# Query-layout heads that keep their exponentials in PSUM, with every low half subtracted on VectorE

## The chip, the cores and the metric

The kernel runs on one core of a Trainium2 chip. A core has a matrix engine (TensorE, PE in the profile, with PEld for its weight loads), a vector engine (VectorE, DVE), an activation engine (ScalarE, ACT), a general engine (GpSimd, POOL) and a queue engine (SyncE, SP) that issues most DMAs here. They run side by side, each in the order of its own program, and wait for one another through semaphores. SBUF is the working memory; PSUM is the memory that TensorE writes its products to. The metric is the time of one execution on the device in microseconds; several runs are taken and the median is used.

## The reference, cut to what matters

Attention over 4 batches of 8 heads, 768 positions, 64 dimensions, in which a query sees only the keys with the same six hash bits; then a gated layer with a spatial product over the positions.

```python
q_bits = (np.einsum('bhsd,dk->bhsk', q, proj) > 0)     # six bits of a position; k_bits likewise
mask = q_bucket[:, :, :, None] == k_bucket[:, :, None, :]
scores = np.where(mask, scale * (q @ k.T), -1e9)
attn = np.exp(scores - scores.max(-1))
x = attn / (attn.sum(-1) + 1e-9) @ v                   # heads side by side: 512 columns
h = np.maximum(x @ w_in, 0)
u, v = h[..., :512], h[..., 512:]
v_n = (v - v.mean(-1)) / np.sqrt(v.var(-1) + 1e-6)
v_s = np.einsum('ts,bsd->btd', w_spatial, v_n) + b_spatial[None, :, None]
out = (u * v_s) @ w_out
```

## The kernel before

There are 32 heads, n = 0 to 31, each with six tiles i of 128 rows. Heads 1 to 7 (`KEYS`) are *key-layout*: their scores come out with the keys on the partitions, their exponentials are used as they are (L265), and a separate pass finds the row maxima (L243). The other 25 heads, 0 and 8 to 31, are *query-layout*, and only they are touched here. The kernel keeps single-precision accuracy by splitting numbers into a 16-bit high part and a 16-bit low part; products are then made of three 16-bit matmuls.

A query-layout tile goes through this ring, all in `scores` and `weighted`:

- L291 and L292 on PE: four matmuls write the scores of 128 queries against 768 keys into a PSUM tile `ps` (`sp` in the trace). The pool `ps_sc` has two such buffers (`PSB[0]`), used in turn by query tiles, key tiles and the row maxima.
- L293 on DVE: the negated row maximum `nb`, with the scaled scores written to a throw-away tile `jk`.
- L295 on ACT: the exponential, from PSUM to an SBUF tile `ex` (three buffers, `EB`).
- L298 on ACT: the high half, `ex` rounded to 16 bits, into `pp[:, 0]` (three buffers, `PB`).
- L299: the low half, `ex` minus the high half, into `pp[:, 1]`. It runs on POOL for tiles 0 and 3 of heads below 16 (`PL_POOL1`) and for tile 2 of the later ones (`PL_POOL`), and on DVE for the others: 34 on POOL, 116 on DVE.
- L301 on SP: one DMA transposes both halves into `pt` (five buffers), so that the keys come to lie on the partitions.
- L314 to L316 on PE: 18 matmuls weigh the values with the transposed tile and add it to the head's sum `pv`.

A main loop over g = 6n + i issues the scores of one tile and the weighted sum of an earlier one (five tiles back, `LAG`), with the preparation of later heads and one or two units of the gating layer in between: `vps` (L361), `ups` (L402), `sps` (L417) and `ops` (L432), twelve or eighteen matmuls each. The gating layer of a batch follows its last head by a queue that is drawn from at a fixed rate of tiles, so the layer of batch 3 comes last, after all heads. The order on each engine isn't that of the text: a scheduler sorts all instructions by priorities that `at` gives and by when their operands are expected, and buffers that are still held count among these.

Of the kernel before, what the change touches and what calls it, by code (L numbers as in the profile page):

```python
# [11 lines left out]
F32 = mybir.dt.float32  # L12
I64 = mybir.dt.int64
U32 = mybir.dt.uint32
AF = mybir.ActivationFunctionType
ALU = mybir.AluOpType
# [3 lines left out]
P = 128  # L20
# [16 lines left out]
def lsh_attention_spatial_gating(  # L37
# [11 lines left out]
    nc = tc.nc  # L49
    B, NPAIR, _, _, S = kq.shape  # L50
    NH = 2 * NPAIR
    NT = S // P
    HS = S // 2
# [4 lines left out]
    ISQ = 1.0 / (SQ * SQ * 8.0)  # L58
# [7 lines left out]
    wk = ctx.enter_context(tc.tile_pool(name="wk", bufs=1))  # L66
# [35 lines left out]
    st = {}  # L102
# [153 lines left out]
    def scores_k(n, i):  # L256
        t = ab[n % NAB]
        ps = ps_sc.tile([P, 2, 512], F32, tag="sc", name=f"sp{n}_{i}")[:, :, :HS]
        ks = slice(i * P, (i + 1) * P)
        for c in range(2):  # L260
            cs = slice(c * HS, (c + 1) * HS)
            nc.tensor.matmul(ps[:, c], lhsT=t[:, 1, ks], rhs=t[:, 0, cs], start=True, stop=False)  # L262
            nc.tensor.matmul(ps[:, c], lhsT=t[:, 2, ks], rhs=t[:, 3, cs], start=False, stop=True)  # L263
        ex = wk.tile([P, S], F32, tag="pt", bufs=PTB, name=f"ex{n}_{i}")
        st["ex", n, i] = nc.scalar.activation(ex.rearrange("p (c q) -> p c q", c=2), ps, AF.Exp, scale=ISQ).ins  # L265
        st["pt", n, i] = ex
# [11 lines left out]
    def scores(n, i):  # L278
        if n in KEYS:
            scores_k(n, i)  # L280
            return
        t = ab[n % NAB]
        if i == 0:
            st["nb", n] = wk.tile([P, NT], F32, tag="nb", bufs=3, name=f"nb{n}")
        nb = st["nb", n][:, i:i + 1]
        jk = wk.tile([P, 2, HS], BF16, tag="jk", name=f"jk{n}_{i}")
        qs = slice(i * P, (i + 1) * P)
        ps = ps_sc.tile([P, 2, 512], F32, tag="sc", name=f"sp{n}_{i}")[:, :, :HS]
        for c in range(2):
            cs = slice(c * HS, (c + 1) * HS)  # L290
            nc.tensor.matmul(ps[:, c], lhsT=t[:, 0, qs], rhs=t[:, 1, cs], start=True, stop=False)  # L291
            nc.tensor.matmul(ps[:, c], lhsT=t[0:P - 1, 3, qs], rhs=t[0:P - 1, 2, cs], start=False, stop=True)  # L292
        nc.vector.tensor_scalar(jk, ps, -ISQ, None, op0=ALU.mult, op1=ALU.min, accum_out=nb)  # L293
        ex = wk.tile([P, 2, HS], F32, tag="ex", bufs=EB, name=f"ex{n}_{i}")
        st["ex", n, i] = nc.scalar.activation(ex, ps, AF.Exp, bias=nb, scale=ISQ).ins  # L295
        at(NT * n + i + G_H, 50)
        pp = wk.tile([P, 2, 2, HS], F16, tag="pp", bufs=PB, name=f"pp{n}_{i}")
        nc.scalar.copy(pp[:, 0], ex)  # L298
        (nc.gpsimd if i in (PL_POOL if n >= 2 * NH else PL_POOL1) else nc.vector).tensor_tensor(out=pp[:, 1], in0=ex, in1=pp[:, 0], op=ALU.subtract)  # L299
        pt = st["pt", n, i] = wk.tile([P, 2 * NT, P], F16, tag="pt", bufs=PTB, name=f"pt{n}_{i}")  # L300
        st["tr"] = nc.sync.dma_start_transpose(out=pt, in_=pp.rearrange("p g c k -> p (g c k)")).ins  # L301

# [144 lines left out]
    N = B * NH  # L447
    NP = B * NPAIR

    PL_POOL = (2,)  # L450
    KEYS = {1, 2, 3, 4, 5, 6, 7}
    PL_POOL1 = (0,3)
    LAGK = 3
    LEAD = 4
    MQ = nc.sync
# [7 lines left out]

    RB = 3
    PB = 3
    EB = 3
    PTB = 5
    XTB = 6
    LAG = 5
# [15 lines left out]
    def at(g, k):  # L485
        tc.cur_priority = int(1000 * (g + 40) + k)
# [17 lines left out]
    for g in range(N * NT + LAG):  # L504
        n, i = divmod(g, NT)
        if n < N:
            at(g + G_S, 0)
            scores(n, i)
            r = n // 2
            at(g + G_P, 300)  # L510
# [103 lines left out]
```

## Time and profile before

| | |
|---|---|
| three runs, median (lowest to highest) | 736.97 us (735.91 to 740.86) |
| span of the profiled execution | 741.7 us |
| head 0 and the key-layout heads 1 to 7 | up to 173 us |
| first score matmul of head 8 to the last subtract of head 31 | 173.0 to 655.6 us |
| the gating layer after the last head, to the end | 660.6 to 741.7 us |

The page lists groups as: line, engine, operation, tile written <- tiles read, shapes, count, then busy time and the mean of one in ns, then how long the engine had been idle just before them and what ended most of that idle time. Rows of waits read: who waited <- for whom: us in total, times, longest. Rows in the order of time begin with the start and the duration in us. In the tables of windows there follow after the window and its length the busy times of PE, weight loads, DVE, ACT and POOL with the counts of instructions, then the granted TensorE clock, the share of the DMA engines' time and GB/s. Names stand without their numbers, so `pp` is any of the three buffers.

### The profile page before, as it was taken

How to read it: one execution, taken by the hardware profiler on the slowest of the kernel's cores; microseconds unless marked ns; L12 is line 12 of the kernel's file. 1: busy time of each engine (PE TensorE's matmuls, PEld its weight loads, DVE VectorE, ACT ScalarE, POOL GpSimd, SP SyncE). 2: the span in 40 equal slices, each digit the busy share in tenths (PEclk: the TensorE clock that was granted, in tenths of full speed). 3: DMA queues.
4: the chain of work that ended last, by engine and by line, in shares of the span. 5: the costliest groups of instructions: out<-in, count | busy, mean ns of one | idle time of the engine just before them, and what ended most of it. 6: DMA issues, size and time to landing. Idle time of an engine off the chain costs nothing.

```text
span 741.7 us, 14927 instructions
## 1 busy us (share of the span) xinstructions
PE 631.5 (85%) x5759; PEld 400.4 (54%) x5759; DVE 520.6 (70%) x945; ACT 434.8 (59%) x668; POOL 321.2 (43%) x324
## 2 busy tenths in 40 slices
PE   1569898998988776997898899889898998999997
PEld 0237686776445444554544555556455565654553
DVE  4677795536799999567689798678698987755200
ACT  1344574346788676655676577667677776743221
POOL 5122443123458675264314565156235571451503
PEclk9768797999999989898999999999999999999999
DMA  9565554324999989996999799999999999860011
GB/s 235 149 123 155 133 148 102 99 55 97 224 237 197 215 207 187 213 178 138 234 202 199 138 210 213 211 211 212 206 210 181 194 175 213 182 136 15 1 42 43
DMA packets 290011, 120.95 MB, mean 163 GB/s; under 512 B 270740, under 2 KB 273812, under 8 KB 289940
## 3 DMA queue, kind: packets, MB, share of 16 engines
q1 hardware_dynamic: 287636, 119.11, 76.4%
q10 hardware_dynamic: 2304, 0.89, 0.5%
q8 instruction: 45, 0.74, 0.4%
q14 instruction: 26, 0.21, 0.1%
HBM read 28.33 MB, written 6.29 MB: 47 GB/s over the span
## 4 chain that ended last, share of the span: by engine, by line
PE 43%; DMA 21%; DVE 13%; issue 8%; ACT 6%; POOL 6%; SPq 3%; ACTq 0%; DVEq 0%; POOLq 0%
DMA pt<-pp 14%; PE pv L275 6%; PE vps L361 6%; PE ops L432 5%; PE sps L417 5%; PE ups L402 5%; DMA ab<-hl 4%; PE sp L291 3%; DVE jk L293 3%; PE sp L292 3%; DVE pp L299 2%; PE sp L262 2%; PE pv L314 2%; ACT ex L295 2%; PE sp L263 2%
## 5 line engine op out<-in xcount | busy, mean ns | idle before, releaser
L295 ACT ACTIVATE ex<-sp,nb 128x768 f32<-128x768 f32 x150 | 134.1, 897 | 54.8 <-DVE jk L293 48.9
L299 DVE TENSOR_TENSOR pp<-ex,pp 128x768 f16<-128x768 f32 x116 | 126.2, 1089 | 47.6 <-ACT pp L298 46.5
L293 DVE TENSOR_SCALAR_CACHE_REDUCE jk<-sp 128x768 bf16<-128x768 f32 x150 | 142.4, 949 | 24.1 <-PE sp L292 22.2
L298 ACT CAST pp<-ex 128x768 f16<-128x768 f32 x150 | 124.3, 829 | 50.0 <-DMA pt<-pp 43.9
L314 PE MATMUL pv<-vp,pt 128*128 128x65 f16 x900 | 108.2, 198 | 40.5 <-DMA pt<-pp 40.2
L291 PE MATMUL sp<-ab 128*128 128x384 f16 x300 | 103.2, 344 | 31.6 <-ACT ex L295 19.3
L314 PEld LDWEIGHTS <-pt 128*128 128x128 f16 x900 | 86.7, 101 | 67.2 <-DMA pt<-pp 53.4
L299 POOL TENSOR_TENSOR pp<-ex,pp 128x768 f16<-128x768 f32 x34 | 58.1, 1708 | 131.1 <-ACT pp L298 124.6
L315 PE MATMUL pv<-vp,pt 128*128 128x64 f16 x900 | 108.0, 197 | 0.0
L316 PE MATMUL pv<-vp,pt 128*128 128x65 f16 x900 | 107.8, 198 | 0.0
L292 PE MATMUL sp<-ab 127*128 127x384 f16 x300 | 103.9, 346 | 0.0
L417 PE MATMUL sps<-ws,vn 128*128 128x384 f16 x576 | 100.9, 329 | 1.5 <-DVE sg L180 1.0
L315 PEld LDWEIGHTS <-pt 128*128 128x128 f16 x900 | 87.0, 100 | 11.3 <-issue 1.3
L316 PEld LDWEIGHTS <-pt 128*128 128x128 f16 x900 | 86.9, 100 | 3.1 <-issue 0.5
L417 PEld LDWEIGHTS <-vn 128*128 128x128 f16 x576 | 55.3, 99 | 37.8 <-issue 3.9
L432 PE MATMUL ops<-wo,g 128*128 128x512 f16 x288 | 70.9, 391 | 1.5 <-ACT o L436 0.9
L275 PEld LDWEIGHTS pv<-vf,ex 128*128 128x128 f32 x504 | 68.5, 208 | 4.1 <-issue 1.6
L402 PE MATMUL ups<-xt,wi 128*128 128x384 f16 x384 | 69.1, 333 | 1.3 <-ACT u L405 0.9
L361 PE MATMUL vps<-wi,xt 128*128 128x512 f16 x288 | 68.0, 383 | 1.4 <-DMA xt<-xs 1.3
L275 PE MATMUL pv<-vf,ex 128*128 128x65 f32 x504 | 67.0, 286 | 0.0
L333 POOL TENSOR_TENSOR x<-x,xf 128x384 f32<-128x384 f32 x32 | 35.5, 1110 | 64.1 <-DVE x L332 64.1
L422 POOL TENSOR_TENSOR sy<-sy,u 128x384 f32<-128x384 f32 x32 | 36.6, 1145 | 49.3 <-DVE sy L421 49.2
(87 smaller groups left out, 1010.7 us busy)
## 6 DMA issues: line engine op xcount, KB each, us to landing
qk<-kq SPq DMA_DIRECT2D x16, 768.0 KB
ab<-hl SPq DMA_DIRECT2D x31, 384.0 KB
ab<-hl SPq DMA_DIRECT2D x34, 192.0 KB
out<-o SPq DMA_DIRECT2D x24, 256.0 KB
v<-v SPq DMA_DIRECT2D x13, 384.0 KB
raw<-w_in SPq DMA_DIRECT2D x16, 256.0 KB
pt<-pp SPq DMA_TRANSPOSE x150
raw<-w_sp SPq DMA_DIRECT2D x12, 192.0 KB
```

The source lines that it names most:

```text
L275: nc.tensor.matmul(acc[:, qi, :], lhsT=ex[:, qi * P:(qi + 1) * P], rhs=vf[p % 2][:, 2 * i + e, :], start=(i == 0 and qi == 0), stop=(i == ...
L291: nc.tensor.matmul(ps[:, c], lhsT=t[:, 0, qs], rhs=t[:, 1, cs], start=True, stop=False)
L292: nc.tensor.matmul(ps[:, c], lhsT=t[0:P - 1, 3, qs], rhs=t[0:P - 1, 2, cs], start=False, stop=True)
L293: nc.vector.tensor_scalar(jk, ps, -ISQ, None, op0=ALU.mult, op1=ALU.min, accum_out=nb)
L295: st["ex", n, i] = nc.scalar.activation(ex, ps, AF.Exp, bias=nb, scale=ISQ).ins
L298: nc.scalar.copy(pp[:, 0], ex)
L299: (nc.gpsimd if i in (PL_POOL if n >= 2 * NH else PL_POOL1) else nc.vector).tensor_tensor(out=pp[:, 1], in0=ex, in1=pp[:, 0], op=ALU.subtract)
L314: nc.tensor.matmul(acc, lhsT=pt[:, c, :], rhs=vh, start=(i == 0 and c == 0), stop=False)
L315: nc.tensor.matmul(acc[:, 0:D], lhsT=pt[:, c, :], rhs=vl, start=False, stop=False)
L316: nc.tensor.matmul(acc, lhsT=pt[:, NT + c, :], rhs=vh, start=False, stop=(i == NT - 1 and c == NT - 1))
L361: nc.tensor.matmul(ps, lhsT=xt[c][:, gx, i * P:(i + 1) * P], rhs=wi[gw][:, c, F2:DF], start=(k == 0), stop=(k == 3 * NPAIR - 1))
L417: nc.tensor.matmul(ps[:, :HS], lhsT=vn[gv][:, c, d * P:(d + 1) * P], rhs=ws[gw][:, c, hs], start=(k == 0), stop=(k == 3 * NT - 1))
```

## The change

For query-layout heads the exponential is written back over the scores in PSUM, the cast and the subtract read it there, and the subtract always runs on DVE (POOL has no access to PSUM, and `PL_POOL`, `PL_POOL1` go). The SBUF tile `ex` and its three buffers go with them. The key-layout heads are as they were.

```diff
         nc.vector.tensor_scalar(jk, ps, -ISQ, None, op0=ALU.mult, op1=ALU.min, accum_out=nb)
-        ex = wk.tile([P, 2, HS], F32, tag="ex", bufs=EB, name=f"ex{n}_{i}")
-        st["ex", n, i] = nc.scalar.activation(ex, ps, AF.Exp, bias=nb, scale=ISQ).ins
+        st["ex", n, i] = nc.scalar.activation(ps, ps, AF.Exp, bias=nb, scale=ISQ).ins
         at(NT * n + i + G_H, 50)
         pp = wk.tile([P, 2, 2, HS], F16, tag="pp", bufs=PB, name=f"pp{n}_{i}")
-        nc.scalar.copy(pp[:, 0], ex)
-        (nc.gpsimd if i in (PL_POOL if n >= 2 * NH else PL_POOL1) else nc.vector).tensor_tensor(out=pp[:, 1], in0=ex, in1=pp[:, 0], op=ALU.subtract)
+        nc.scalar.copy(pp[:, 0], ps)
+        nc.vector.tensor_tensor(out=pp[:, 1], in0=ps, in1=pp[:, 0], op=ALU.subtract)
```

Lines behind L295 stand one lower in the changed kernel: the exponential is L294, the cast L297, the subtract L298, the transpose L300, and the weighted sums L313 to L315.

With the same priorities the scheduler sorts differently, since a score buffer is now held to the end of the subtract. On DVE, in head 16 before (`jk16_5` is the row maximum of head 16, tile 5; `pp16_4` the subtract of tile 4; `rv` and `x` normalize an earlier head):

```order
L293 TENSOR_SCALAR jk16_4_4164,nb16_3997<-sp16_4_4165 128x768
L328 TENSOR_SCALAR rv15_4200<-pv15_3978 128x6
L293 TENSOR_SCALAR jk16_5_4213,nb16_3997<-sp16_5_4214 128x768
L329 RECIPROCAL rv15_4200<-rv15_4200 128x6
L330 SCALAR_TENSOR_TENSOR rv15_4200<-nb15_3702,rv15_4200 128x6
L332 TENSOR_TENSOR x15_4204<-pv15_3978,rv15_4200 128x384
L293 TENSOR_SCALAR jk17_0_4277,nb17_4276<-sp17_0_4278 128x768
L299 TENSOR_TENSOR pp16_4_4173<-ex16_4_4171,pp16_4_4173 128x768
```

The same place in the changed kernel:

```order
L293 TENSOR_SCALAR jk16_4_4106,nb16_3943<-sp16_4_4107 128x768
L298 TENSOR_TENSOR pp16_3_4083<-sp16_3_4076,pp16_3_4083 128x768
L298 TENSOR_TENSOR pp16_4_4114<-sp16_4_4107,pp16_4_4114 128x768
L293 TENSOR_SCALAR jk16_5_4154,nb16_3943<-sp16_5_4155 128x768
L293 TENSOR_SCALAR jk17_0_4217,nb17_4216<-sp17_0_4218 128x768
L219 SCALAR_TENSOR_TENSOR vp1_95<-v32_9_3705,vp1_95 128x12x64
L298 TENSOR_TENSOR pp16_5_4162<-sp16_5_4155,pp16_5_4162 128x768
```

Before, the row maxima of the next two tiles stood ahead of a tile's subtract; now at most that of the next one does, and the subtracts come in pairs behind pairs of maxima.

On PE, behind the last weighted sum of the last head (`pv31`, from `pt31_5`), before (`g2` and `ops2_3` belong to the gating layer of batch 2):

```order
L315 MATMUL pv31_8675<-vp1_95,pt31_5_8673 128x64
L316 LDWEIGHTS pt31_5_8673
L316 MATMUL pv31_8675<-vp1_95,pt31_5_8673 128x65
L432 LDWEIGHTS g2_1_1_8389
L432 MATMUL ops2_3_8801<-wo0_106,g2_1_1_8389 128x512
```

The same place now (`xt15` holds the last pair of heads, `vps3_0` opens the gating layer of batch 3):

```order
L314 MATMUL pv31_8525<-vp1_95,pt31_5_8523 128x64
L315 LDWEIGHTS pt31_5_8523
L315 MATMUL pv31_8525<-vp1_95,pt31_5_8523 128x65
L360 LDWEIGHTS xt15_8647
L360 MATMUL vps3_0_8699<-wi0_102,xt15_8647 128x512
```

All of batch 2's layer now stands ahead of the last head's weighted sums, and so do the first nine of twelve matmuls of `vps3_0` and of `vps3_1`; before, 28 matmuls of `ops2_3` to `ops2_5` and all 72 of `vps3` stood behind.

More of the change, by code (lines that the diff above doesn't have):

```diff
@@ L448, in lsh_attention_spatial_gating @@
     NP = B * NPAIR
-    PL_POOL = (2,)
     KEYS = {1, 2, 3, 4, 5, 6, 7}
-    PL_POOL1 = (0,3)
     LAGK = 3
@@ L465, in lsh_attention_spatial_gating @@
     PB = 3
-    EB = 3
     PTB = 5
```

## Prediction

> **What bounds the kernel now.** I read the page's totals first, then the busy times of the long stage, then its groups and waits, and last single tiles in the order of time. A tile below is one block of 128 queries of a query-layout head; there are 150, six for head 0 and 144 for heads 8 to 31.
>
> ```profile
> span 741.7 us, 14927 instructions
> PE 631.5 (85%) x5759; PEld 400.4 (54%) x5759; DVE 520.6 (70%) x945; ACT 434.8 (59%) x668; POOL 321.2 (43%) x324
> 173.00:656.00 483.00, 417.36 (x4331) 258.02 (x4330) 394.94 (x704) 334.85 (x499) 240.80 (x219) 0.95 0.98 197
> ```
>
> The last row is the window 173 to 656 us, in which all 144 tiles run: PE is busy 417.4 of 483 us (86%), VectorE (DVE) 394.9 (82%), ScalarE (ACT) 334.9 (69%), POOL 240.8 (50%), and the DMA engines 98%. Nothing is idle enough to be called free, and DMA is nearest to full. The same window by groups and by waits:
>
> ```profile
> L293 DVE TENSOR_SCALAR_CACHE_REDUCE jk<-sp 128x768 bf16<-128x768 f32 x144 | 136.7, 949 | 19.6 <-PE sp L292 17.7
> L295 ACT ACTIVATE ex<-sp,nb 128x768 f32<-128x768 f32 x144 | 128.8, 897 | 40.6 <-DVE jk L293 34.7 <-issue 3.2 <-DMA ab<-sg 0.7
> L299 DVE TENSOR_TENSOR pp<-ex,pp 128x768 f16<-128x768 f32 x112 | 122.4, 1094 | 47.5 <-ACT pp L298 46.5 <-issue 0.3
> L298 ACT CAST pp<-ex 128x768 f16<-128x768 f32 x144 | 119.3, 829 | 49.8 <-DMA pt<-pp 43.9 <-ACT ex L295 1.3 <-ACT g L423 1.2
> L299 POOL TENSOR_TENSOR pp<-ex,pp 128x768 f16<-128x768 f32 x32 | 54.3, 1696 | 110.6 <-ACT pp L298 104.1 <-DVE jk L293 5.6 <-PE vps L361 0.9
> PE pv L314 <- DMA pt<-pp: 34.5, 29, 4.0
> PE sp L291 <- ACT ex L295: 18.9, 15, 5.1
> ```
>
> The reader sees a ring with two limits. The cast L298 waits 43.9 us for a transpose to give one of three pp buffers back, and PE 34.5 us for transposed tiles: that is the DMA side. PE waits only 18.9 us, 15 times, for an exponential to give a score buffer back: that is the PSUM side, so far nearly free. One tile with hardly a wait shows the links; the last row is the first matmul of the tile two later, which takes the same score buffer:
>
> ```profile
> 515.47 0.33 PE L291 MATMUL sp<-ab 128*128 128x384 f16 x1
> 516.76 0.95 DVE L293 TENSOR_SCALAR_CACHE_REDUCE jk<-sp 128x768 bf16<-128x768 f32 x1
> 517.92 0.89 ACT L295 ACTIVATE ex<-sp,nb 128x768 f32<-128x768 f32 x1
> 518.84 0.83 ACT L298 CAST pp<-ex 128x768 f16<-128x768 f32 x1
> 519.83 0.95 DVE L299 TENSOR_TENSOR pp<-ex,pp 128x768 f16<-128x768 f32 x1
> 520.53 0.32 PE L291 MATMUL sp<-ab 128*128 128x384 f16 x1
> ```
>
> Today the buffer is free when L295 ends, 517.92 + 0.89 - 515.47 = 3.34 us after it was taken. The matmul at 520.53 starts before the subtract ends at 520.78: that order is what the change forbids.
>
> **The change, step by step.** *The hold.* The score buffer is now released by the subtract, not by the exponential. There are two score buffers, so the time per tile cannot be under (hold + handover) / 2, where the hold runs from the first score matmul to the end of the subtract. First, last and an early undisturbed tile of the 144:
>
> ```profile
> 173.01 0.33 PE L291 MATMUL sp<-ab 128*128 128x384 f16 x1
> 177.33 1.64 POOL L299 TENSOR_TENSOR pp<-ex,pp 128x768 f16<-128x768 f32 x1 [9.53 <-ACT pp L298]
> 174.73 0.33 PE L291 MATMUL sp<-ab 128*128 128x384 f16 x1
> 180.38 1.16 DVE L299 TENSOR_TENSOR pp<-ex,pp 128x768 f16<-128x768 f32 x1
> 648.58 0.32 PE L291 MATMUL sp<-ab 128*128 128x384 f16 x1
> 654.48 1.11 DVE L299 TENSOR_TENSOR pp<-ex,pp 128x768 f16<-128x768 f32 x1
> ```
>
> From 173.01 to 654.48 + 1.11 = 655.59 it is 482.6 us, or 3.35 us a tile; so two buffers allow a hold of 6.7. Over the 144 tiles (first and last above) the distance from matmul to end of subtract is now 9.38 us on average, far over 6.7; 1.67 us of it is the cast's wait, mostly for pp. In the 32 tiles whose cast follows the exponential within 0.1 us (first 174.73, last 648.58) it is 6.83. The subtract averages 1.23 us over all 144, and 0.95 undisturbed (row at 519.83), so I take 6.83 - 0.33 = 6.50 for a tile that does not wait for pp (its own subtract averaged 1.28 there and takes 0.95). Bounds for the new hold: 5.31 (the tile at 515.47) gives 2.7 us a tile and costs nothing; 9.38 - 0.28 = 9.10 gives 4.58 and costs 1.23 x 144 = 177 us. The truth lies between: waits on PE, DVE and ACT are partly slack that a tighter order removes, but the wait for pp does not go while DMA is 98% full. I take 6.50 plus half of the 1.67, 7.34, plus 0.05 for the handover: 3.70 us a tile, so 144 x (3.70 - 3.35) = **+50 us**, nearer the lower end because 6.50 comes from whole tiles of the same kernel. Behind the waiting score matmul on PE stand the weighted sums and the gating matmuls, which wait with it; behind those, SP issues the next heads' loads in the same order as the transposes, so they slip too and cost nothing more.
>
> The Trainium skill, Perfetto Trace Analysis, Identifying Performance Opportunities, says that the same gap repeating on an engine that should be saturated can mean too few SBUF or PSUM buffers for the next tile. That speaks against this change. The trace bears it out only weakly so far, with the 18.9 us above; by the rule that row should grow several times over.
>
> *The operations.* The nearest rows for new operand places:
>
> ```profile
> L332 DVE TENSOR_TENSOR x<-pv,rv 128x384 f32<-128x384 f32 x32 | 17.8, 555 | 0.7
> L339 DVE TENSOR_TENSOR xs<-x,xs 128x384 f16<-128x384 f32 x32 | 20.1, 628 | 3.7 <-ACT xs L338 3.7
> L405 ACT ACTIVATE u<-ups 128x384 f32<-128x384 f32 x32 | 15.5, 486 | 10.5 <-PE ups L402 9.6 <-PE pv L316 0.8
> L423 ACT CAST g<-sy 128x384 f16<-128x384 f32 x32 | 16.3, 508 | 39.7 <-POOL sy L422 37.1 <-DMA ab<-sg 2.6
> L265 ACT ACTIVATE ex<-sp 128x768 f32<-128x768 f32 x42 | 33.9, 806 | 32.2 <-PE sp L263 28.9 <-PE mp L241 3.0
> 652.28 1.81 DVE L299 TENSOR_TENSOR pp<-ex,pp 128x768 f16<-128x768 f32 x1
> 652.27 1.00 POOL L333 TENSOR_TENSOR x<-x,xf 128x384 f32<-128x384 f32 x1 [0.51 <-DVE x L332]
> ```
>
> A DVE product from PSUM (L332) takes 0.555 us where the one from SBUF (L339) takes 0.628, and the subtract at 652.28 took 1.81 beside a POOL operation against 0.95 alone. So the subtract from PSUM is 0.95, bounded by 0.95 and 1.09. All 144 on DVE make 144 x 0.95 = 137 us instead of 122.4, +14; DVE's stage goes from 395 to 409 us, hidden as long as the tile time is 3.70 (DVE then 77% of 532), and up to 14 us if it is not. POOL loses 54.3 us; it waited 104.1 us for casts, so that is worth nothing by itself. The cast from PSUM: 0.83, less some 0.02 by L405 against L423, nothing. No row shows ACT writing PSUM: 0.90 as now, bounded by 0.81 (L265, without bias) and, as much above, 0.99; that is 0.09 of hold, 0.045 a tile, 6 us either way.
>
> The Trainium skill, Perfetto Trace Analysis, Optimizing Scalar/DVE Operations, gives DVE about 60 ns of access overhead on SBUF and about 125 ns on PSUM. By that the 144 subtracts would cost 144 x 65 ns, an estimate of 9 us of DVE more. L332 and L339 show no such surcharge, so the sum leaves it out.
>
> *The end.* The scheduler also moves gating matmuls. After the last weighted sum stand now:
>
> ```profile
> 660.58 6.04 PE ops L432 x28
> 666.62 15.54 PE vps L361 x72
> ```
>
> In the changed order the 28 output matmuls of batch 2 stand ahead of the last head's weighted sums, and so do 18 of the 72 that open batch 3. On the chain that ends last that is 6.04 + 18 x 15.54 / 72 = 9.9 us less; it goes into PE's idle time of the long stage (483 - 417 = 66 us). If that cover is gone it comes back whole. **-10 us**. Head 0's six tiles, by the same 0.35 us: **+2 us** (bounds 0 and 7, by 1.23 a tile).
>
> The sum is +42 us on the profiled execution's 741.7, or 783.7. The three runs have a median of 736.97 (735.91 to 740.86), 4.7 under that span; taking it off gives 779, which I round to **778**.
>
> **The rivals.** (a) *Hidden behind the transposes.* For it: DMA at 98%, 43.9 us of pp waits; a score chain that is slower where it would have waited anyway costs nothing. Against: the hold has to stay at 6.6 or less, and unhurried tiles already need 6.5. The tile time stays at 3.35 to 3.45: -8 to +6 us, 729 to 743.
>
> (b) *Faster.* 59 of the 116 DVE subtracts run beside a POOL tensor operation and average 1.22 us against 0.95 for the rest, and 34 run on POOL at 1.7. Taking this away shortens the way from cast to transpose by 59 x 0.27 + 34 x 0.75 = 41 us in total, and with three pp buffers the ring turns 41 / 3 = 14 us faster if pp is the limit; with the end's 10 that makes about 714. It decides only while the mean hold stays under 2 x 3.35 - 0.05 = 6.65 us. The Trainium skill, SBUF — State Buffer, Who interferes with whom, has the mechanism: a DVE instruction with two SBUF inputs contends with a GpSimd one that reads SBUF, one with at most one SBUF input does not. The row at 652.28 agrees.
>
> (c) *DVE becomes the bound.* 409 us at today's share of 82% make the stage 500 us, +17; with the end, 746. Against: the two-buffer ring bites first.
>
> (d) *All waits stay.* Hold 9.10, 4.58 us a tile, +177 - 8: 906. Against: slower tiles leave every engine less loaded, which shortens its queues.
>
> **How the numbers follow.** The forecast, the two-buffer ring at 3.4 to 4.0 us a tile, 742 to 825, has 0.66; (a) 0.12, (b) 0.06, (c) 0.08, (d), in full or for the larger part, 0.08. One per cent is 7 us, about what a measurement of this kernel can tell from no change. Faster by more than that (under 730): (b) and a little of (a), 0.08. Within: most of (a) and a corner of the forecast and (c), 0.10. Slower: 0.82. The range that leaves out (b), some of (a) and the worse half of (d) is 735 to 845.
>
> **What would show it.** PE's wait at L291 for the subtract (it was 18.9 us, for the exponential) should be the largest PE wait, 60 us or more; the tile time in the long stage 3.7 us; the cast's wait for pp down to half of 43.9; DMA share near 0.88 there; the subtract near 0.95 us and no longer stretched; the end 10 us shorter after the last weighted sum. It is wrong if PE's wait at L291 stays under 30 us, if DMA stays at 0.98, or if the exponential into PSUM costs clearly more than 0.99.

## The result: 12% slower, and the profile after

The changed kernel takes 825.64 us (median of 4 runs, 822.47 to 828.68) against 736.44 us (also of 4 runs, one more than in the table above); the ratio is 1.121, with a 95% interval of 1.116 to 1.126. The forecast was slower, 778 us; the time lies within its range, but the loss is 89 us where 42 were forecast. The page of the changed kernel, first its totals:

```profile
span 824.4 us, 14923 instructions
PE 666.0 (81%) x5759; PEld 410.2 (50%) x5759; DVE 520.1 (63%) x979; ACT 433.9 (53%) x668; POOL 228.5 (28%) x290
```

Every engine is a smaller share of the span than before. TensorE alone has clearly more busy time, matmuls 666.0 against 631.5 us and weight loads 410.2 against 400.4, with the same 5759 of each. So it isn't the load of one engine; something makes all of them wait. The ends of the long stage, first score matmul of head 8 and last subtract of head 31, with the window between:

```profile
177.00 0.33 PE L291 MATMUL sp<-ab 128*128 128x384 f16 x1
738.59 0.96 DVE L298 TENSOR_TENSOR pp<-sp,pp 128x768 f16<-128x768 f32 x1 [1.77 <-ACT pp L297]
177.00:740.00 563.00, 458.81 (x4423) 271.98 (x4422) 395.48 (x737) 337.93 (x504) 157.69 (x190) 0.89 0.82 171
```

The stage now takes 739.55 - 177.00 = 562.6 us, 3.91 us a tile, against 482.6 and 3.35. That is +80 of the span's +82.7; the start has +4.0, the end -1.3. The DMA engines fell from 98% to 82%: they are no longer near full. The stage by groups and by waits:

```profile
L293 DVE TENSOR_SCALAR_CACHE_REDUCE jk<-sp 128x768 bf16<-128x768 f32 x144 | 137.1, 952 | 78.2 <-PE sp L292 74.7 <-PE pv L315 1.1
L298 DVE TENSOR_TENSOR pp<-sp,pp 128x768 f16<-128x768 f32 x144 | 136.7, 952 | 43.4 <-ACT pp L297 42.9
L294 ACT ACTIVATE sp<-sp,nb 128x768 f32<-128x768 f32 x144 | 126.0, 876 | 115.0 <-DVE jk L293 114.4
L297 ACT CAST pp<-sp 128x768 f16<-128x768 f32 x144 | 114.8, 799 | 17.0 <-ACT sp L294 4.8 <-issue 3.3 <-DMA ab<-sg 3.2
PE pv L313 <- DMA pt<-pp: 67.6, 48, 4.1
PE sp L291 <- DVE pp L298: 31.8, 25, 3.6
ACT pp L297 <- DMA pt<-pp: 2.8, 4, 1.1
```

Each of the four operations is as fast as before (the row maximum within 3 ns) or faster. What grew is the waiting for the link before: VectorE 74.7 us for scores (17.7 before), ScalarE 114.4 for the maximum (34.7). The cast hardly waits for a pp buffer any more (2.8 us, last row; 43.9 before). Read from the end backwards, everybody waits for TensorE to make the next scores. But TensorE itself waits only 31.8 us for a released buffer, and 67.6 for transposes. The answer is in what it does between a release and the next scores:

```profile
620.35 0.96 DVE L298 TENSOR_TENSOR pp<-sp,pp 128x768 f16<-128x768 f32 x1 [1.93 <-ACT pp L297]
...
621.04 2.77 PE L401 MATMUL ups<-xt,wi 128*128 128x384 f16 x8
623.60 0.26 PE L313 MATMUL pv<-vp,pt 128*128 128x65 f16 x1
...
624.10 0.51 PE L291 MATMUL sp<-ab 128*128 128x384 f16 x1
...
625.57 0.33 PE L291 MATMUL sp<-ab 128*128 128x384 f16 x1
```

The subtract of tile 4 of head 26 ends at 621.31 and frees its score buffer. On TensorE eight gating matmuls are in front, then weighted sums, then the scores of the other buffer at 624.10, late for the same reason; the freed buffer is used again at 625.57, 4.26 us after it was free. The matmuls also run slowly there, 0.51 us where 0.33 is usual. From this example the three questions of the experiments: is it the two score buffers at all; is it TensorE's order and its waits between release and next use (the *handover*); or is it TensorE's clock?

Over all 144 tiles the hold (first score matmul to end of subtract) is 6.13 us and the handover (end of subtract to the first score matmul two tiles later) 1.67, each as a mean over the trace from the first to the last row above. Their sum over two, 3.90, is the tile time, as two buffers used in turn require. In the average handover TensorE runs 0.72 us of gating matmuls, 0.51 of the other buffer's scores and 0.23 of weighted sums, and is idle for 0.15. This queue was there before the change: in the kernel before, where the end of the exponential frees the buffer, the same means are a hold of 5.11 us and a handover of 1.56.

### The profile page after: what moved, and what is told of

It is laid out like the page before. It is cut to its first block, busy times and chain, and to the rows that moved or that the text cites. A ratio compares the mean times of both kernels' runs of the same rounds, so it can differ in the third digit from the quotient of the medians.

```text
span 824.4 us, 14923 instructions
## 1 busy us (share of the span) xinstructions
PE 666.0 (81%) x5759; PEld 410.2 (50%) x5759; DVE 520.1 (63%) x979; ACT 433.9 (53%) x668; POOL 228.5 (28%) x290
## 4 chain that ended last, share of the span: by engine, by line
PE 46%; DMA 24%; DVE 14%; ACT 7%; issue 6%; SPq 1%; POOL 1%; ACTq 1%; DVEq 0%; POOLq 0%
DMA pt<-pp 17%; PE sps L416 8%; PE ups L401 6%; PE ops L431 5%; PE vps L360 5%; PE pv L275 4%; DVE pp L298 4%; PE sp L291 3%; DVE jk L293 3%; PE sp L292 3%; PE pv L313 2%; ACT sp L294 2%; DMA raw<-w_sp 2%; ACT pp L297 2%; PE pv L315 2%
## 5 line engine op out<-in xcount | busy, mean ns | idle before, releaser
L294 ACT ACTIVATE sp<-sp,nb 128x768 f32<-128x768 f32 x150 | 131.3, 876 | 132.3 <-DVE jk L293 131.6
L313 PE MATMUL pv<-vp,pt 128*128 128x65 f16 x900 | 112.0, 204 | 73.6 <-DMA pt<-pp 73.6
L298 DVE TENSOR_TENSOR pp<-sp,pp 128x768 f16<-128x768 f32 x150 | 142.4, 952 | 44.5 <-ACT pp L297 44.0
L291 PE MATMUL sp<-ab 128*128 128x384 f16 x300 | 111.9, 373 | 46.1 <-DVE pp L298 31.8
L313 PEld LDWEIGHTS <-pt 128*128 128x128 f16 x900 | 89.8, 104 | 107.4 <-DMA pt<-pp 99.2
L297 ACT CAST pp<-sp 128x768 f16<-128x768 f32 x150 | 119.6, 799 | 17.2 <-ACT sp L294 4.8
L292 PE MATMUL sp<-ab 127*128 127x384 f16 x300 | 113.2, 377 | 0.1
L315 PE MATMUL pv<-vp,pt 128*128 128x65 f16 x900 | 111.8, 204 | 0.0
L314 PEld LDWEIGHTS <-pt 128*128 128x128 f16 x900 | 90.6, 104 | 7.5 <-issue 1.2
L315 PEld LDWEIGHTS <-pt 128*128 128x128 f16 x900 | 90.9, 104 | 2.2 <-issue 0.3
L360 PE MATMUL vps<-wi,xt 128*128 128x512 f16 x288 | 71.8, 401 | 7.5 <-DMA xt<-xs 6.8
L291 PEld LDWEIGHTS <-ab 128*128 128x128 f16 x300 | 32.2, 107 | 73.9 <-DVE pp L298 40.2
L265 ACT ACTIVATE ex<-sp 128x768 f32<-128x768 f32 x42 | 33.9, 806 | 44.4 <-PE sp L263 39.5
```

The source lines that it names most:

```text
L294: st["ex", n, i] = nc.scalar.activation(ps, ps, AF.Exp, bias=nb, scale=ISQ).ins
L297: nc.scalar.copy(pp[:, 0], ps)
L298: nc.vector.tensor_tensor(out=pp[:, 1], in0=ps, in1=pp[:, 0], op=ALU.subtract)
L313: nc.tensor.matmul(acc, lhsT=pt[:, c, :], rhs=vh, start=(i == 0 and c == 0), stop=False)
L314: nc.tensor.matmul(acc[:, 0:D], lhsT=pt[:, c, :], rhs=vl, start=False, stop=False)
L315: nc.tensor.matmul(acc, lhsT=pt[:, NT + c, :], rhs=vh, start=False, stop=(i == NT - 1 and c == NT - 1))
```

## The experiments

Theory A: the longer hold of two score buffers makes the loss, and TensorE's queue adds the handover. Theory B: TensorE's waits let its granted clock fall, and the slow matmuls make much of the loss. Theory C: the operations themselves cost it, VectorE's 34 more subtracts or the operands in PSUM.

**Only the engine of the subtract.**

```diff
-        (nc.gpsimd if i in (PL_POOL if n >= 2 * NH else PL_POOL1) else nc.vector).tensor_tensor(out=pp[:, 1], in0=ex, in1=pp[:, 0], op=ALU.subtract)
+        nc.vector.tensor_tensor(out=pp[:, 1], in0=ex, in1=pp[:, 0], op=ALU.subtract)
```

> The kernel before with one part of the change alone: all subtracts on VectorE, the exponentials still in SBUF, so that the score buffer is free after the exponential as before. Theory A (the longer hold of the score buffer makes the loss): 730 to 750 us, DMA share in the long stage near 0.97, cast waits for pp still 30 us or more. Theory C (VectorE's added subtracts make it): 770 us or more, VectorE near 90% busy in the long stage.

734.65 us, ratio to the kernel before 0.996 (0.993 to 0.999): a small gain, and no loss. Its waits:

```profile
PE sp L291 <- ACT ex L295: 16.7, 20, 1.7
ACT pp L298 <- DMA pt<-pp: 33.6, 29, 3.0
```

Theory C falls for VectorE's load: the 34 subtracts cost nothing here. The cast's waits for pp are still there, 33.6 us of them; the last kernels take them up.

**Only the hold.** In the same kernel the subtract also takes a pointer operand out of the score buffer, which its first operation then ignores. The exponentials stay in SBUF.

```diff
+        nc.vector.scalar_tensor_tensor(out=pp[:, 1], in0=ex, scalar=ps[:, 0, 0:1], in1=pp[:, 0], op0=ALU.bypass, op1=ALU.subtract)
```

> The kernel before with all subtracts on VectorE and the exponentials in SBUF, but the subtract takes a pointer operand out of the score buffer that it does not use, so that the buffer is held until the subtract ends. The hold alone, without PSUM as place of the exponentials. Theory A: as slow as the changed kernel or slower, 815 to 850 us, since the subtract can again be stretched by POOL. Theory C, or a cost of the PSUM operands: under 770 us.

837.69 us, ratio 1.135 (1.129 to 1.140). Between this kernel and the last one stands one pointer operand, and with it the time at which the score buffer is released; it costs 103 us. The scheduler sorts anew for it, so that TensorE's matmuls stand in another order than in the last kernel: the 103 us are the price of the longer hold with the order that comes with it, and no run holds the buffer longer in the old order. The exponentials' place in PSUM is no cost; the changed kernel is 12 us faster than this one (825.6 against 837.7). Its subtract takes 0.95 us on average, against 1.10 here, which may be the reason; it was not tested by itself.

**A third score buffer.** To make room for it in PSUM, the pools of the weighted sums and of the small tiles give up one buffer each, and a second kernel pays that price alone.

```diff
-    PSB = (2,2,2)
+    PSB = (3,1,1)
```

> The changed kernel with three score buffers; to make room in PSUM the weighted sums and the small tiles have one buffer each in place of two. To be read against the next kernel, which pays the same price with two score buffers. Theory A (two score buffers, their hold and handover, set the pace): at least 50 us under the next one, and TensorE's wait for the subtract under 10 us. If TensorE's own order, its waits for transposes and its clock set the pace whatever the buffers: within 15 us of the next one.

```diff
-    PSB = (2,2,2)
+    PSB = (2,1,1)
```

> The changed kernel with one buffer each for the weighted sums and the small tiles and still two for the scores: the price of the smaller pools alone. 840 to 920 us by every theory; it is the base for the three score buffers.

757.71 us with three, 831.50 with two: 74 us from the third buffer, again with the order that the scheduler makes for it. TensorE's waits, first with three buffers, then with two:

```profile
PE pv L313 <- DMA pt<-pp: 33.9, 38, 4.4
PE sp L291 <- DVE pp L298: 11.7, 13, 2.2
```

```profile
PE pv L313 <- DMA pt<-pp: 75.1, 59, 3.7
PE sp L291 <- DVE pp L298: 19.1, 24, 2.0
```

With three the stage takes 467.7 us, 3.25 a tile, under the kernel before, though a tile holds its buffer for 8.24 us: a longer hold does no harm when a buffer is to spare. The whole is slower than the kernel before because of the end: 127 us from the last subtract, where it is 108 with the same small pools and two score buffers, and 85 in the changed kernel. Two expectations were a little off: the base was to be 840 us or more, and the remaining wait under 10 us. The wait for transposes halves together with the ring's: with two buffers it is a consequence of the ring at least in part. The next kernels take that up.

**TensorE's order.** A gating unit may no longer stand ahead of the score matmuls of the step that issues it.

```diff
+        st["mm"] = mm.ins
...
             while queue and credit >= 1.0:
-                queue.pop(0)()
+                with tc.issue_after(st["mm"]):
+                    queue.pop(0)()
```

> The changed kernel with one more order: a unit of the gating layer may not stand on TensorE ahead of the score matmuls of the step that issues it. If gating matmuls ahead of the next score matmul are what lengthens the handover (1.67 us a tile in the changed kernel): handover about 1.2 us, 785 to 810 us. If not: within 1% of the changed kernel.

813.18 us, handover 1.17: the handover came out as expected, the time 3 us above the range named, since the hold rose to 6.37. The order takes 12 us off. What it would take off the kernel before was not run, so these are not shown to be 12 us of the loss.

**TensorE without waits for transposes**, alone and together with that order. In the edit above `mm` is the last score matmul of the step; here `ptc` is a constant tile, made in two more lines that are not shown, so that the lines below stand two lower.

```diff
-        pt = st.pop(("pt", n, i))
+        st.pop(("pt", n, i))
+        pt = ptc
```

> The changed kernel, but the weighted sums read one constant tile in place of the transposed exponentials, which are still made and transposed; this leaves the weighing by the attention out of the result. TensorE then never waits for a transpose. If those waits (73.6 us of TensorE in the changed kernel) and the half clock that follows such gaps are what lies on the path: 730 to 765 us and time at half clock near 100 us. If the ring of two score buffers sets the pace by its hold and the gating matmuls ahead of the next scores: 790 to 825 us, with TensorE's wait for the subtract growing from 32 us to 80 or more.

785.29 us, handover 1.19. It lies between the two expectations: without TensorE's waits for transposes the kernel is 40 us faster (33 of them in the long stage), and the rest stays, with more waiting for the subtract, though not the 80 us that were named:

```profile
PE sp L293 <- DVE pp L300: 55.6, 32, 7.0
```

> The changed kernel with both edits on TensorE's side: the weighted sums read a constant tile (which leaves the weighing by the attention out of the result), and no gating unit stands ahead of the score matmuls of its step. If the handover of the score buffer is made of waits for transposes and of gating matmuls ahead of the scores: handover under 1.0 us and 750 to 775 us. If it is made of something else: 780 us or more, as with the constant tile alone (785).

763.07 us, handover 0.75, stage 512.6 us. So the two edits on TensorE's side together take 63 us off (50 of them in the long stage), and the handover falls from 1.67 to 0.75. What is left of the stage's loss, 512.6 - 482.6 = 30 us, is the hold (6.35 us) with what remains of the handover: together 7.10, where 6.70 would be 3.35 us a tile. The kernel before waits for transposes too (34.5 us in its long stage), and neither edit was made to it; so the runs show what shortens the handover and what that is worth here, and not how the 89 us divide.

**TensorE's clock.** The mean granted clock over the span, changed kernel and kernel before:

```profile
core 0: 824.4 us, clock 0.881
```

```profile
core 0: 741.7 us, clock 0.937
```

The clock records of both traces hold no other value than 1.0 and 0.5, so that is 2 x 0.119 x 824.4 = 196 us at half clock, against 2 x 0.063 x 741.7 = 93. Such a difference could be the cause as well as a trace of it. So the waits were filled with matmuls that nobody reads:

```diff
...
+            if c == 0 and i > 0:
+                for _ in range(8):
+                    nc.tensor.matmul(st["pvw", n][:, 390:512], lhsT=ident, rhs=ident[:, 0:122], start=False, stop=False)
```

> The changed kernel with eight matmuls of 122 columns, whose product nobody reads, ahead of every weighted sum of a query-layout tile but the first of a head: 125 x 8 matmuls of about 0.05 us, 50 us of TensorE work that should fall into its waits. Theory B (the half clock that follows TensorE's waits makes a large part of the loss): time at half clock falls from 197 us to 130 or less and the time falls to 780 to 815 us. If the clock only follows the loss: 830 to 870 us.

834.25 us in the profiled run and 849.08 in the other, both above the changed kernel's 825.64. The profiled run's clock:

```profile
core 0: 832.5 us, clock 0.926
```

Time at half clock falls to 2 x 0.074 x 832.5 = 123 us, most of the way back, and the kernel gets slower, not faster. The filler has a price of its own: TensorE's busy time rises from 666.0 to 696.9 us, and it stands ahead of scores too (handover 1.84). So this run alone doesn't tell what the clock is worth. The kernel with two score buffers and smaller pools says more. Its long stage, inside this window, has nearly the clock of the kernel before (0.93, against 0.95), and takes 549.6 us, 67 more than there:

```profile
170.00:721.00 551.00, 446.71 (x4426) 269.68 (x4426) 391.18 (x737) 337.10 (x505) 156.56 (x190) 0.93 0.85 174
```

Theory B falls as the main cause: a loss of that size is there, in the long stage of this kernel, almost without the low clock. How many microseconds the clock adds in the changed kernel stays open.

**Versions that are faster than both.** If the transposes' buffers limit the kernel before, a fourth pp buffer should help; it was paid for with one of the three SBUF buffers of the exponentials. With all subtracts on VectorE, with the low halves on POOL as before, and with VectorE and the paced order:

```diff
-    PB = 3
-    EB = 3
+    PB = 4
+    EB = 2
```

> The kernel before with all subtracts on VectorE, exponentials in SBUF in two buffers in place of three, and four pp buffers in place of three. If the pp buffers still limit the kernel (ScalarE's cast waited 43.9 us for them before): 715 to 730 us. If the transposes' own rate does: 730 to 740 us.

728.47 us, ratio 0.984 (0.978 to 0.989).

> The kernel before, low halves on POOL as they were, with four pp buffers and two for the exponentials in SBUF. If the fourth pp buffer alone makes the gain of the kernel that has it with all subtracts on VectorE: 724 to 732 us. If both parts are needed: 734 us or more.

725.61 us, ratio 0.982 (0.974 to 0.991): the pp buffer does it without moving the subtracts. ScalarE's wait for pp, 43.9 us in the kernel before, is now:

```profile
ACT pp L298 <- DMA pt<-pp: 3.6, 4, 1.5
```

> The kernel before with all subtracts on VectorE, four pp buffers, two for the exponentials in SBUF, and the order that keeps a gating unit behind the score matmuls of its step. Where the score buffer is free early (handover below zero) the order should bring little: 720 to 735 us.

722.08 us, ratio 0.978 (0.970 to 0.987), the fastest of all; the three intervals overlap, so their order among themselves isn't settled. The expectation counts the handover from the subtract; from the exponential, which frees the buffer here, it is 1.77 us.

## Why the prediction was right and where it was wrong

*The ring of two buffers.* The mechanism was right: the longer hold alone and the third buffer show it, each with the order that comes with it. The tile time was to be 3.70 us and is 3.91, which is 30 us over 144 tiles and most of the miss. The step that failed is "plus 0.05 for the handover". The prediction saw what stands behind the waiting score matmul on TensorE, not what stands ahead of it: a released buffer is worth nothing until the matmuls in front have run, and these are gating matmuls, the other buffer's scores and weighted sums, which may have waited for their transposes. The handover is 1.67 us. The trace of the kernel before showed it: weighted sums or gating matmuls stood in 134 of the 143 gaps between one tile's scores and the next one's, and the handover after the exponential was 1.56 us. It had only to be priced.

*The hold.* It was to be 7.34 us, 6.50 and half of the wait for pp. It is 6.13: the waits inside the ring fell with the load, and the pp wait went to nearly nothing. This error had the other sign: 1.21 / 2 x 144 = 87 us too much, against 1.62 / 2 x 144 = 117 us too little for the handover; the difference is the 30 us. With the hold right and the handover at 0.05 the ring would have come to 3.09 us a tile, less than before, and the forecast to no loss at all. And with the hold as it was taken and the 1.56 us that could be read, it would have come to 4.45 us a tile, far too much. The direction was right for a reason that was only half seen, and that the time lies inside the range owes something to luck, two errors of opposite sign.

*The rest of the miss.* Of the 48 us between 778 and 825.64, the ring makes 30, the end 9 (below) and the start 2. About 6 come from the span that the sum began with: the profiled execution of the kernel before was 5 us above its median, that of the changed kernel 1 below. The last 1 is a slip, as 779 was rounded to 778. Another slip is the time given to the forecast, 742 to 825: 3.4 to 4.0 us a tile with the other terms of the sum are 736 to 823.

*The operations.* Right: subtract 0.952 us (0.95 taken), none longer than 0.96, VectorE's load hidden (395.5 us in the stage, where 409 were expected with old contention in the rest). The exponential into PSUM takes 0.876 us, inside its bounds of 0.81 to 0.99, the cast from PSUM 0.799. The row at 519.83, taken as undisturbed, isn't quite: by the profile a POOL addition with both operands in SBUF starts 0.16 us after it. The value holds all the same, since the 57 VectorE subtracts of the kernel before that run beside no POOL tensor operation average 0.952.

*The end.* Forecast 10 us shorter, measured 0.8 from the last weighted sum (1.3 from the last subtract). The order did move 46 matmuls ahead of the last weighted sums, but the 28 of batch 2 had been covering something:

```profile
744.71 0.57 DVE x L331
745.41 0.99 POOL x L332
747.56 3.21 DMA xt<-xs
750.82 1.46 PE L360 MATMUL vps<-wi,xt 128*128 128x512 f16 x3 [6.78 <-DMA xt<-xs]
750.82 13.99 PE vps L360 x54
```

After the last weighted sum the last head is normalized and transposed, and the gating layer of batch 3 needs it. Before, the output matmuls from 660.58 to 666.62 hid this; now TensorE is idle for 6.78 us, and its next 54 matmuls take 13.99 us, 0.26 each, against 15.54 / 72 = 0.22 before, 2.3 us more for the 54. Together these give back 9.1 of the 9.9 us. The step that failed counted the moved matmuls and left out what they covered.

*What was to show it.* The wait at L291 for the subtract was to be 60 us or more and to be the largest; it is 31.8, less than the 67.6 for transposes, because the ring's time went into the handover while TensorE was busy or waiting for transposes. The DMA share fell further than named (0.82 against 0.88), and so did the cast's wait for pp (2.8 us against 22). Rival (a) fell although the hold of 6.13 stayed under its limit of 6.6: the limit holds for hold plus handover, 7.80. Rival (b) fell for the same reason. Its premise on POOL was right as to the subtract, which is no longer stretched, but all subtracts on VectorE with the old hold are only 3 us faster, where it counted 14 for the ring. (c) fell: VectorE is 70% busy in the stage. (d), at 906, was too much: most of the waits inside the hold did not stay, since it fell to 6.13 us.

## What to carry to other kernels

When a buffer is to be held longer, take (hold + handover) / buffers against the present time per tile. Read the handover from the present trace, from the step that frees the buffer now to the refill, and see what fills it: everything that stands in the queue of the refilling engine, with the waits of that work. Hold plus handover over the buffers is the tile time in every kernel that uses its buffers in turn, so the sum by itself does not show that the buffers limit; one buffer more does. An engine that shows little waiting for the buffer may still be the one that is late, since it is busy with what stands in front. Before counting work that moves off the end of a chain as gain, look for what it covers there.

## What the runs showed of the hardware that was not expected

- TensorE at a granted mean of 0.881 took 666.0 us for the same 5759 matmuls that took 631.5 us at 0.937. Filling its waits raised the clock to 0.926 and did not shorten the kernel (834.25 us against 825.64).
- ScalarE is a little faster with PSUM in place of SBUF: exponential 0.876 us into PSUM against 0.897 into SBUF, cast 0.799 us from PSUM against 0.829 from SBUF. The Trainium skill, PSUM — Partial Sum Buffer, Specifications (TRN2), says that ScalarE writes faster to PSUM than to SBUF; the trace agrees, with 21 ns.
- A VectorE subtract with one operand in PSUM takes 0.952 us, as the one with both in SBUF does beside no POOL tensor operation (0.952, the mean of 57 in the kernel before).
